# Fifteen loads of 15, 14, ... 1 short rows between the first bulk loads of a decode kernel

## Chip, cores, metric

One core of one Trainium2 chip. The metric is the device time of one execution in microseconds (us); lower is better. A row of numbers for a kernel is the median of its runs. "Landing" is the moment at which one DMA engine reports its part of a load; a load over k engines has k landings, and the trace records each (16 for a 128-row load). The packet records carry no engine number; where an engine is followed, it is by packets that join end to start.

## The reference

One decode step of a transformer block, batch 1, bfloat16: layer norm, attention of one query token over a cache of 4,096 positions in 32 heads of 128, output projection, residual, layer norm, a gated MLP (640 to 1,728 to 640), residual.

```python
h  = x + attention(layernorm(x), k_cache, v_cache, wq, wo)     # k_cache, v_cache: 1 x 32 x 4096 x 128
h2 = h + (gelu(n @ w_gate) * (n @ w_up)) @ w_down              # n = layernorm(h)
```

The inputs are 84.2 MB, each byte used once, so the kernel is a stream of loads with compute behind it.

## The kernel before

All loads are issued by the sync queue (SP), with one semaphore each. The K and V caches come in eight turns of 4 MB each, into two slots. Each of the 16 DMA engines moves eight rows of a 128-row load: at the start of the trace the packets join into sixteen chains of eight rows of 40,960 bytes, eight of 16,384, and so on.

```python
def load(name, dst, src):
    SP.dma_start(dst, src).then_inc(S[name], 16)

def load_kv(which, m, tiles, src, free):      # cut: waits, slot arithmetic
    if (which, m) in (("k", 0), ("k", NQ - 1), ("v", NQ - 1)):
        for h in range(2):                    # in two halves
            r = slice(h * NB // 2, (h + 1) * NB // 2)
            load(f"{which}{slot}{'ab'[h]}", tiles[slot][:, r, :], src[:, r, :])
    else:
        load(f"{which}{slot}a", tiles[slot], src)
# ... cut ...
load("wq", wq_sb, A_wq.rearrange("(p c) n -> p c n", c=DC))            # 128 rows of 40,960 bytes
SP.wait_ge(S["dve"], DVE_X4)
load("x", x4[0:P:32, :], A_x[0, 0].rearrange("(r d) -> r d", r=YR))    # 4 rows of 320 bytes
for m in range(NQ):                           # NQ = 8
    load_k(m)
    if m in (0, 2, 4):
        load_wo(m // 2)                       # 128 rows of 10,240 bytes
    if m == 1:
        SP.wait_ge(S["q"], 1)
    load_v(m)
load_wo(TURNS - 1)
load("wg", wg_sb, B_w_gate.rearrange("(p c) f -> p c f", c=DC))
# ... cut: the up weights in two loads, then the down weights ...
load("wd0", wd_last, B_w_down[FULL * P : DF, :].rearrange("(p b) d -> p b d", b=PER))  # 32 rows
```

At the end GpSimd (POOL) puts the semaphores back, while the output store is under way:

```python
spare(DVE).then_inc(S["all"], 1)
POOL.wait_ge(S["all"], 1)
POOL.sem_inc(S["pe"], -done["pe"])
# ... cut: five more ...
for name in [*once, "x"]:                     # ten names
    POOL.sem_inc(S[name], -16)
ACT.wait_ge(S["out"], 16)
ACT.sem_inc(S["out"], -16)
```

The softmax here doesn't subtract the row's maximum and nothing guards it: scores larger than these inputs give would overflow.

## Time and profile before

| | before |
|---|---|
| time, median of 6 runs | 206.29 us (206.16 to 207.57) |
| span of the profiled run | 204.6 us |
| time after the span's end, same run | 1.65 us |
| 32,768-byte row on one engine, mean | 1.219 us |
| first V load, 16 landings: first / mean / last | 37.58 / 38.00 / 39.57 us |
| last down-projection load, landings: first / mean / last | 199.16 / 200.14 / 201.00 us |
| GpSimd's closing list, first reset to its last no-op | 1.28 us |

The page of the kernel before: the span, its 40 slices of DMA business (tenths) and rate, the packets, two of the queues, and the chain of waits that ended last.

```profile
span 204.6 us, 7392 instructions
...
DMA  7999999999999999999999999999999999999990
GB/s 248 408 420 439 416 471 413 448 434 426 413 416 425 435 426 436 448 429 416 429 436 406 458 442 436 416 423 436 448 429 416 413 423 432 432 420 424 405 366 34
DMA packets 4394, 84.38 MB, mean 412 GB/s; under 512 B 512, under 2 KB 512, under 8 KB 928
...
q1 hardware_dynamic: 4384, 84.23, 96.7%
q8 instruction: 8, 0.13, 0.3%
...
## 4 chain that ended last, share of the span: by engine, by line
DMA 16%; PE 7%; SPq 1%; DVE 0%; issue 0%
DMA big<-in_B_w_down_dram 16%; SPq L510 1%; PE tp_104 L252 1%; PE tp_105 L252 1%; PE tp_106 L252 1%; PE tp_107 L252 1%; PE sa L265 1%; PE sb L265 1%; PE a L288 0%; PE tp_106 L439 0%; DVE y_row L686 0%; PE o L300 0%; DVE spare L169 0%; PE o 
```

The DMA engines are busy in practically every slice, and what the chain of waits ends in is a load. The page's "instruction" queues I take for the program itself being fetched. It goes through the same engines: seven packets of 16 KB between 32 and 76 us took 1.02 to 1.09 us each, and while one is under way fifteen row packets are in flight in place of sixteen.

Stretches of the span, same kernel. Columns: stretch, its length, busy time of five engines with counts, granted clock, DMA share, GB/s.

```profile
...
core 0: us, PE busy (x) PEld busy (x) DVE busy (x) ACT busy (x) POOL busy (x), PEclk, DMA share, GB/s
...
15.00:40.00 25.00, 17.28 (x248) 12.63 (x248) 11.38 (x36) 7.75 (x8) 0.64 (x1) 0.93 1.02 438
40.00:120.00 80.00, 65.41 (x1549) 64.22 (x1545) 28.45 (x55) 38.81 (x88) 8.34 (x4) 0.72 1.00 428
120.00:190.00 70.00, 58.67 (x1514) 56.88 (x1511) 23.56 (x48) 34.73 (x83) 4.49 (x2) 0.73 1.00 429
```

The last column is the one to read: 428 to 438 GB/s in mid-stream.

The end of the chain in order of time (start, duration, what):

```profile
...
168.47 32.53 DMA big<-in_B_w_down_dram
201.00 0.04 issue
201.04 0.47 PE tp_106 L439 x8
201.51 0.02 issue
201.53 0.33 DVE y_row L686
```

The last landing, half a microsecond of matmuls, the add. After that come the output store and the closing handshake. Who ended the sync queue's own waits in that handshake (total, times, longest):

```profile
...
engine line waited for: us in total, times, longest us
...
SPq L158 <- ACTq L158: 0.6, 1, 0.6
```

It is the scalar queue, which waits for the output store. GpSimd's list (1.28 us) is done about 0.45 us sooner and costs nothing.

### The profile page before, as it was taken

Reading aid. Unit: us, or ns where it says so; the run is one execution under the profiler, and the core shown is the slowest. Engines: PE = TensorE matmul, PEld = TensorE weight load, DVE = VectorE, ACT = ScalarE, POOL = GpSimd, SP = SyncE. Lnnn points to the kernel's source line nnn. Section 1 sums busy time; section 2 is a strip of 40 time slices with the busy share of each in tenths; the row PEclk is TensorE's granted clock in tenths of the full one; section 3 lists DMA queues with packets and bytes.
Section 4 is the critical chain, followed back from the end, with each engine's and each line's share of the span. In section 5 each row is a group of like instructions: output and inputs, shape, how many; then the busy total and the mean of one; then the engine's idle time right before and its main releaser. Section 6 shows DMA issues by size and latency. Waiting matters only on the chain. (4 is left out here: it accounts for less than half of the span.)

```text
span 204.6 us, 7392 instructions
## 1 busy us (share of the span) xinstructions
PE 148.9 (73%) x3415; PEld 137.1 (67%) x3415; DVE 71.6 (35%) x180; ACT 81.5 (40%) x179; POOL 19.2 (9%) x17
## 2 busy tenths in 40 slices
PE   0001949945996499889984998199869989986743
PEld 0001239945996499889974997199859979986321
DVE  2006026600471038206601750047107703802660
ACT  0000035543285317535660557027715672870000
POOL 8300000350000000710000035000000000000000
PEclk9999987975597559957975797559757976985575
DMA  7999999999999999999999999999999999999990
GB/s 248 408 420 439 416 471 413 448 434 426 413 416 425 435 426 436 448 429 416 429 436 406 458 442 436 416 423 436 448 429 416 413 423 432 432 420 424 405 366 34
DMA packets 4394, 84.38 MB, mean 412 GB/s; under 512 B 512, under 2 KB 512, under 8 KB 928
## 3 DMA queue, kind: packets, MB, share of 16 engines
q1 hardware_dynamic: 4384, 84.23, 96.7%
q8 instruction: 8, 0.13, 0.3%
q14 instruction: 2, 0.02, 0.0%
HBM read 84.23 MB, written 0.00 MB: 412 GB/s over the span
## 5 line engine op out<-in xcount | busy, mean ns | idle before, releaser
L278 PE MATMUL o<-ex,big 128*128 128x4 bf16 x1024 | 29.9, 166 | 10.1 <-ACT ex L574 6.3
L278 PEld LDWEIGHTS o<-ex,big 128*128 128x128 bf16 x1024 | 28.5, 103 | 11.4 <-ACT ex L574 7.5
L560 ACT COPY big<-tp_105 128x1024 bf16<-128x1024 bf16 x16 | 16.2, 1012 | 46.4 <-PE tp_105 L252 46.4
L252 PE MATMUL tp_104<-ident,big 128*128 128x128 bf16 x256 | 24.1, 250 | 10.6 <-PEq L177 10.6
L252 PEld LDWEIGHTS tp_104<-ident,big 128*128 128x128 bf16 x256 | 19.6, 115 | 11.0 <-issue 11.0
L252 PE MATMUL tp_105<-ident,big 128*128 128x128 bf16 x256 | 24.0, 248 | 0.0
L252 PE MATMUL tp_106<-ident,big 128*128 128x128 bf16 x256 | 23.4, 245 | 0.0
L505 POOL COPY wo<-wo_in 128x5120 bf16<-128x5120 bf16 x3 | 13.4, 4451 | 105.3 <-PE a L288 105.3
L587 DVE COPY big<-tp_104 128x1024 bf16<-128x1024 bf16 x24 | 16.5, 688 | 18.2 <-PE tp_104 L252 18.2
L252 PE MATMUL tp_107<-ident,big 128*128 128x128 bf16 x256 | 22.5, 238 | 0.0
L252 PEld LDWEIGHTS tp_105<-ident,big 128*128 128x128 bf16 x256 | 19.6, 114 | 0.0
L252 PEld LDWEIGHTS tp_106<-ident,big 128*128 128x128 bf16 x256 | 19.3, 113 | 0.0
L252 PEld LDWEIGHTS tp_107<-ident,big 128*128 128x128 bf16 x256 | 18.5, 109 | 0.0
L265 PE MATMUL sb<-q_78,big 128*128 128x4 bf16 x512 | 14.4, 164 | 4.5 <-issue 4.5
L587 DVE COPY big<-tp_107 128x1024 bf16<-128x1024 bf16 x24 | 16.6, 691 | 2.9 <-PE tp_107 L252 2.5
L560 ACT COPY big<-tp_106 128x1024 bf16<-128x1024 bf16 x16 | 16.2, 1014 | 3.3 <-PE tp_106 L252 3.3
L265 PEld LDWEIGHTS sb<-q_78,big 128*128 128x128 bf16 x512 | 13.7, 97 | 4.6 <-issue 4.6
L574 ACT ACTIVATE ex<-sa 32x64 bf16<-32x64 f32 x32 | 9.8, 306 | 11.4 <-PE sa L265 11.2
L587 DVE COPY big<-tp_106 128x1024 bf16<-128x1024 bf16 x16 | 11.1, 692 | 8.4 <-PE tp_106 L252 8.1
L265 PE MATMUL sa<-q_78,big 128*128 128x4 bf16 x512 | 14.0, 164 | 0.0
L265 PEld LDWEIGHTS sa<-q_78,big 128*128 128x128 bf16 x512 | 13.5, 96 | 0.6
L644 DVE COPY o_raw<-o 128x4 f32<-128x4 f32 x4 | 0.7, 163 | 35.8 <-PE o L278 35.8
(118 smaller groups left out, 114.4 us busy)
## 6 DMA issues: line engine op xcount, KB each, us to landing
big<-in_A_v_cache_dram SPq DMA_DIRECT2D x7, 4096.0 KB, 33.0
big<-in_A_k_cache_dram SPq DMA_DIRECT2D x6, 4096.0 KB, 26.6
big<-in_A_k_cache_dram SPq DMA_DIRECT2D x4, 2048.0 KB, 22.0
big<-in_A_wq_dram SPq DMA_DIRECT2D x1, 5120.0 KB, 15.2
wo_in<-in_A_wo_dram SPq DMA_DIRECT2D x4, 1280.0 KB, 25.9
big<-in_A_v_cache_dram SPq DMA_DIRECT2D x2, 2048.0 KB, 28.3
big<-in_B_w_gate_dram SPq DMA_DIRECT2D x1, 2160.0 KB, 37.8
big<-in_B_w_up_dram SPq DMA_DIRECT2D x1, 1728.0 KB, 41.6
```

Source lines behind the costliest of these rows:

```text
L252: inst = PE.transpose(tp_b[g % NBANK][:, b * DH : (b + 1) * DH], kt[slot][:, g * GRP + b, :], ident[:])
L265: inst = PE.matmul(s_ps[half][:, j % (NB // 2), :], lhsT=kt[slot][:, j, :], rhs=q8[:, slot * QH : (slot + 1) * QH], start=True, stop=True,)
L278: inst = PE.matmul(o_ps, lhsT=vt[slot][:, j, :], rhs=e_t[:, j, :], start=(j == 0), stop=(j == NB - 1))
L505: POOL.tensor_copy(wo_t[:], wo_in[:]).then_inc(S["wo"], 1)
L560: ACT.copy(group(m % SLOTS, g), tp_g[g % NBANK]).then_inc(S["act_pe"], 1)
L574: inst = ACT.activation(e_t[r, cols, i], s_ps[half][r, :, i], AF.Exp, scale=SCALE, accum_out=rs_all[r, half, h : h + 1])
L587: DVE.tensor_copy(group(m % SLOTS, g), tp_g[g % NBANK]).then_inc(S["dve_pe"], 1)
L644: event(DVE.tensor_copy(o_raw[:, HG * turn : HG * turn + QH], o_ps))
```

## The change

Fifteen loads, one of 15 rows, one of 14, ... one of 1 row, each row 1,152 bytes, written to scratch space that nobody reads. The intent is a stagger. In the trace of the change a load of k short rows has k landings and one early jump (16 events for 15 rows, 2 for one row), and the loads share their engines: the 42 short packets of the first bunch can be followed as thirteen engines with three of them, one with two, one with one and one with none. Engine e has 15 - e short rows to do and is meant to fall behind by so many steps, so that the engines no longer start their bulk rows together. They stand in four bunches (3, 3, 4 and 5 loads) between the first five bulk loads.

```diff
-        + ["x", "wq", ..., "wd3", "out"]
+        + ["x", "wq", ..., "wd3", "out"] + [f"mark{k}" for k in range(1, 16)]
@@ load_kv
                 load(f"{which}{slot}{'ab'[h]}", tiles[slot][:, r, :], src[:, r, :])
+                if (which, m, h) == ("k", 0, 0):
+                    mark_loads(12, 11, 10)
@@ the order of loads
+    marks = part(2 * SLOTS * TILE + W_MLP, W_MLP)
+
+    def mark_loads(*ks):
+        for k in ks:
+            load(f"mark{k}", marks[0:k, (k - 1) * 576 : k * 576], A_wq[0:k, 0:576])
+
+    mark_loads(15, 14, 13)
     for m in range(NQ):
         load_k(m)
         if m in (0, 2, 4):
+            mark_loads(*{0: (9, 8, 7, 6)}.get(m, ()))
             load_wo(m // 2)
+            mark_loads(*{0: (5, 4, 3, 2, 1)}.get(m, ()))
         if m == 1:
             SP.wait_ge(S["q"], 1)
         load_v(m)
     load_wo(TURNS - 1)
     load("wg", wg_sb, ...)
+    for k in range(1, 16):
+        SP.wait_ge(S[f"mark{k}"], 16)
@@ GpSimd's closing list
-    for name in [*once, "x"]:
+    for name in [*once, "x"] + [f"mark{k}" for k in range(1, 16)]:
+        POOL.wait_ge(S[name], 16)
         POOL.sem_inc(S[name], -16)
```

More of the change, by code (lines that the diff above doesn't have):

```diff
@@ L153 @@
         [f"{t}{i}{h}" for t in "kv" for i in range(SLOTS) for h in "ab"]
-        + ["x", "wq", "wo", "wo_in", "wg", "wu0", "wu1", "wd0", "wd1", "wd2", "wd3", "out"]
+        + ["x", "wq", "wo", "wo_in", "wg", "wu0", "wu1", "wd0", "wd1", "wd2", "wd3", "out"] + [f"mark{k}" for k in range(1, 16)]
         + ["pe", "dve", "act", "pool", "q", "dve_pe", "act_pe", "y", "all"]
```

## The prediction

> **What bounds the kernel now.** The load stream. The page's slices show DMA busy 9 tenths nearly throughout, 412 GB/s on average; the chain of waits ends in 32.5 us of the last down-projection load (16% of the span), then 0.47 us of matmuls, the add and the store. Packet records: a 32,768-byte row takes 1.219 us in the mean, 26.9 GB/s on one engine. [...] In mid-stream each 4 MB load lands 9.72 us after its predecessor, whatever the engines' phases: I see no collision there for a stagger to remove. Excess packet time sits in the first row (about 0.66 us per engine, before any mark), in seven instruction fetches between 32 and 76 us, each setting one engine back by 1.0 us, and at 193 to 196 us (about 0.5 us per engine).
>
> So the engines are spread already: the last load's 16 landings run from 199.16 to 201.00 us, and the last one counts.
>
> **What the change does.** [...] the 4-partition x load agrees: 4 packets, 4 landings and one earlier jump. Loads of 15, 14, ... 1 rows thus give engine 0 fifteen small rows and engine 15 none. One costs, by estimate from rows of 320 (19 ns), 2,560 (102) and 10,240 bytes (385), 50 ns for 1,152 bytes plus 8 ns for the semaphore write: 58 ns. Engine 0 is set back by 0.87 us, engine 8 by 0.4, for good, because the stream never pauses.
>
> Issue: a DMA costs the queue 0.4 to 0.65 us, so fifteen add 7 to 9 us before the first second-slot load (now 4.3 us). The first load alone keeps the engines busy until 15 us, so nothing starves. The fifteen waits before the up weights are long satisfied.
>
> Tail: GpSimd resets semaphores at the end, 0.078 us each, done at 203.2 us; the rest waits for the output store until 203.69. Fifteen more resets cost 1.17 us plus little for waits, so GpSimd ends last, at about 204.4. Less the 0.45 us of slack, about 0.75 us lands on the end.
>
> **On the critical path.** Last landing +0.6 us (one of the lowest four engines already has a fetch and a late start, and gets 0.7 to 0.87 more; the worst engine's number I cannot tell), tail +0.75 us. Sum +1.3 us, 0.6%. The crowding at 193 to 196 us may change by 0.3 us either way.
>
> **Predicted: 207.6 us, range 206.8 to 208.5.** Faster by over 2%: 0.01; within 2%: 0.97; slower: 0.02.
>
> **What would show it.** (a) 120 packets of 1,152 bytes, about 50 ns each. (b) Bulk rows unchanged at 1.219 us, 9.72 us per 4 MB load. (c) Mid-stream landings of one load spread over more than the present 1.8 us, the first landing unmoved. (d) Last down-projection landing near 201.6 us. (e) GpSimd's resets ending 1.2 us later relative to the output add, the closing handshake waiting on GpSimd.
>
> **What would make it wrong.** If the fetches hit high-numbered engines, the ramp evens the engines out and the last landing stays or falls by up to 0.5 us (206.5). If each small load stalls its engine for its semaphore write's round trip (0.4 us from data to landing), engine 0 loses several us: 210. If waits and resets take an instruction each, the tail is 2.5 us longer.

That the stream is the bound rests on the page alone (DMA slices, chain of waits). +0.6 us for the last landing and +0.75 us for the tail make the +1.3 us.

## More of the kernel before

A "completion" is the end of a load's part on one engine, where its semaphore is raised (in the traces a packet of 4 bytes, 9 ns, behind the engine's last row).

## The result

| | before | after |
|---|---|---|
| time, median | 206.35 us (20 runs) | 210.15 us (10 runs, 209.87 to 211.39) |
| span of the profiled run | 204.6 us | 208.8 us |
| time after the span's end, same run | 1.65 us | 2.14 us |
| 32,768-byte row, mean | 1.219 us | 1.219 us |
| first V load, landings: first / mean / last | 37.58 / 38.00 / 39.57 us | 38.52 / 39.46 / 40.59 us |
| last down-projection load, landings | 199.16 / 200.14 / 201.00 us | 200.29 / 201.69 / 203.50 us |
| 1,152-byte row, mean of 120 | none | 107 ns (51 to 336) |
| GpSimd's closing list | 1.28 us | 2.89 us |

The ratio is 1.018, 95% interval 1.016 to 1.020. A ratio is the mean time of one kernel's fast runs over that of the other's fast runs of the same rounds, so it is not quite the ratio of the medians. The change is slower, clear of the noise, by just under 2%. The profiled run (210.90 us) is one of the slower ones of its kernel, 0.75 us over the median.

The page after:

```profile
span 208.8 us, 7429 instructions
...
DMA  6989999999999999999999999999999999999950
GB/s 251 455 358 403 395 450 424 425 433 430 424 436 409 436 419 452 421 427 452 427 404 448 410 458 427 421 433 446 421 433 436 399 430 430 419 433 425 378 217 2
DMA packets 4635, 84.53 MB, mean 405 GB/s; under 512 B 632, under 2 KB 752, under 8 KB 1168
...
q1 hardware_dynamic: 4624, 84.37, 95.5%
q8 instruction: 8, 0.13, 0.3%
...
## 4 chain that ended last, share of the span: by engine, by line
DMA 15%; PE 7%; SPq 1%; DVE 0%; issue 0%
DMA big<-in_B_w_down_dram 15%; SPq L510 1%; PE tp_104 L252 1%; PE tp_105 L252 1%; PE tp_107 L252 1%; PE tp_106 L252 1%; PE sa L265 1%; PE sb L265 1%; PE a L288 0%; PE tp_106 L439 0%; PE o L300 0%; DVE y_row L699 0%; DVE spare L169 0%; PE o 
```

The added packets (241 more, 0.15 MB more) are far too few bytes to account for the loss. Single slices mislead here: the third has fallen from 420 to 358 GB/s, but the second has risen from 408 to 455. Stretches:

```profile
...
core 0: us, PE busy (x) PEld busy (x) DVE busy (x) ACT busy (x) POOL busy (x), PEclk, DMA share, GB/s
...
15.00:40.00 25.00, 16.75 (x243) 12.28 (x244) 11.29 (x36) 7.75 (x8) 0.53 (x1) 0.93 1.02 418
40.00:120.00 80.00, 64.03 (x1503) 62.84 (x1501) 25.89 (x50) 36.85 (x85) 8.45 (x4) 0.70 1.00 428
120.00:190.00 70.00, 59.29 (x1531) 57.90 (x1528) 25.12 (x47) 36.77 (x85) 4.49 (x2) 0.78 1.00 430
```

The loss is in 15 to 40 us alone: 418 for 438 GB/s, and 20 GB/s over 25 us are 0.5 MB, which at 430 GB/s is 1.2 us. From 40 to 190 us the stream runs exactly as before: 428 for 428, 430 for 429. So the stagger costs while it is made and neither gains nor loses later.

The end of the chain, and the waits of the sync queue in the closing handshake:

```profile
...
171.38 32.12 DMA big<-in_B_w_down_dram
203.50 0.04 issue
203.54 0.46 PE tp_106 L439 x7
204.00 0.02 issue
204.03 0.32 DVE y_row L699
```

```profile
...
engine line waited for: us in total, times, longest us
...
SPq L158 <- POOLq L158: 1.2, 1, 1.2
...
SPq L158 <- ACTq L158: 0.5, 1, 0.5
```

The chain has the same links, 2.5 us later (e2 below, profiled at its median, has 1.8 us for the loads alone). But the handshake now waits 1.2 us for GpSimd, which in the kernel before it never waited for. The two losses are separate, a stream loss and a tail loss, and the first experiments divide them.

### The profile page after: what moved, and what is told of

It is laid out like the page before. It is cut to its first block, busy times and chain, and to the rows that moved or that the text cites. A ratio compares the mean times of both kernels' runs of the same rounds, so it can differ in the third digit from the quotient of the medians.

```text
span 208.8 us, 7429 instructions
## 1 busy us (share of the span) xinstructions
PE 148.9 (71%) x3415; PEld 137.4 (66%) x3415; DVE 71.7 (34%) x180; ACT 81.6 (39%) x179; POOL 19.2 (9%) x17
## 5 line engine op out<-in xcount | busy, mean ns | idle before, releaser
L310 PE MATMUL o<-x_col,mean_f 128*128 128x10 f32 x2 | 0.6, 376 | 17.2 <-DVE x_col L208 17.2
```

Of the source, the lines that this page charges most:

```text
L310: mark("moments", PE.matmul(ps, lhsT=mean_f[:], rhs=rhs, start=True, stop=True))
```

## The experiments

Eighteen kernels, each timed in five rounds against the kernel before; all gave correct results. By times alone none is 2% slower than the kernel before (at most 1.4%, e6), and the 95% interval of a ratio is about 0.7 us to either side. Finer differences are therefore read from landings, of one profile per kernel. "d" is the median less the median of before. Landings are quoted as first / mean / last of 16. In the texts of expectation a kernel is named without its number.

A note on the times. Every kernel, the one before included, has a second group of runs about 1.1 us above the first (before: mostly 206.1 to 206.9, some at 207.5 to 208.0). In most profiles of slower runs the last thing to finish is not the load but the compute behind it: in e9, e11, e13, e14, e16 and e18 the output add starts 1.3 to 2.8 us after the last landing, in all the others 0.4 to 0.5 us. The change's own profile is an exception: it is 0.75 us over the median with an add 0.53 us after the last landing, so there the landings themselves were late. The chain of e13_own8_four, whose profile fell in the upper group, reads

```profile
...
## 4 chain that ended last, share of the span: by engine, by line
PE 15%; DVE 4%; ACT 4%; issue 1%
PE tp L252 9%; ACT ex L593 4%; PE o L278 2%; PE sa L265 2%; PE tp L439 1%; PE a L288 1%; DVE g_col L669 0%; DVE u_col L669 0%; PE tp L310 0%; PE tp L300 0%; DVE h_col L207 0%; DVE rs_w L221 0%; DVE rs_w L222 0%; DVE rs_y L224 0%; PE o L300 
```

with TensorE's granted clock at 0.50 from 190 to 200 us, and no DMA in the chain's summary. The clock is not shown to be the cause: it is 0.50 there in e10's profile too, which is of the lower group. No profile of the kernel before fell into its upper group, so that its runs there are the same thing is inferred. Where a median hops between groups (e13, e16), I compare landings or the groups, not medians.

### Dividing tail and stream: e1_resets_only, e2_loads_only

e1 leaves the fifteen loads out and raises their semaphores by hand; e2 keeps the loads and resets their semaphores on the sync queue.

```diff
# e1                                              # e2
     def mark_loads(*ks):                              for k in range(1, 16):
-        for k in ks: load(...)                            SP.wait_ge(S[f"mark{k}"], 16)
+        pass                                     +    for k in range(1, 16):
+    for k in range(1, 16):                       +        SP.sem_inc(S[f"mark{k}"], -16)
+        SP.sem_inc(S[f"mark{k}"], 16)            # GpSimd's closing list as before
```

> The fifteen loads are left out; their semaphores are raised by the sync queue at about 153 us instead, and the longer list of waits and resets at the end of GpSimd stays. If the tail and the stream are separate terms, this costs the tail alone: in the changed kernel GpSimd's list took 2.89 us against 1.28, less about 0.45 us of slack, so +1.2 us, 207.5 us, with the last down-projection landing still near 201.0 us and its spread 1.8 us. Rival: the longer tail is an accident of the profile (0.4 us of it was a late sync drain) and the time moves by the +0.75 us of the prediction or less, 207.1 us.

> The fifteen loads stay as they are; their semaphores are reset by the sync queue after its fifteen waits at about 154 us, and GpSimd's end is that of the kernel before. The stream's share alone: last landing near 203.5 us instead of 201.0, so +2.3 to +2.6 us, 208.8 us. Together with the resets alone it should make the whole +3.8 us. If the prediction's 58 ns a load were right and the rest were tail, it would be 207.0 us.

Measured: e1 208.66 us (d +2.17), last landing 201.25; e2 208.12 us (d +1.63), landings of the first V load 38.42 / 39.40 / 40.59, last landing 202.83. 2.17 + 1.63 = 3.80, and the whole change costs 210.15 - 206.35 = 3.80. The two terms add (to the hundredth by luck: e2's six runs reach from 207.70 to 208.75), and the tail is the larger. The waits of the sync queue in the handshake, e1 and then e2:

```profile
...
SPq L158 <- POOLq L158: 1.2, 1, 1.2
```

```profile
...
SPq L158 <- ACTq L158: 0.6, 1, 0.6
```

Both texts missed the sizes: e1 cost 1 us more than I had worked out of the profile, e2 0.7 us less. What the profile of the span could not show is that e1's runs also end later after the span: 2.21 us on average against 1.70 of before, and 1.67 in e2.

### The tail: e8_pool_early, e16_resets_padded

```diff
# e8: GpSimd, after its third copy at about 115 us, not in the closing list
+    for k in range(1, 16):
+        POOL.wait_ge(S[f"mark{k}"], 16)
+        POOL.sem_inc(S[f"mark{k}"], -16)
+    spare(POOL).then_inc(S["pool"], 1)
# ... and the sync queue, in place of its fifteen waits
+    SP.wait_ge(S["pool"], POOL_ALL)
# e16: e1 and, on the sync queue at about 154 us,
+    for _ in range(15):
+        SP.sem_inc(S["mark1"], 1)
+        SP.sem_inc(S["mark1"], -1)
```

> The fifteen loads as in the change; GpSimd waits for and resets their semaphores after its third copy (about 115 us) instead of at the end, then tells the sync queue, which waits once. If the tail's +2.2 us came from GpSimd's list standing at the end, it is gone: 208.1 us as with the loads alone, and the time after the last counted instruction is 1.6 us again, not 2.2. If it came from GpSimd's program being longer [...], it stays: 209.5 us or more.

> resets_only (208.66 us) with thirty more semaphore instructions on the sync queue at about 154 us, where it has time. Fetch theory [...]: the extra fetch of 8 KB moves to about 160 us, the drain that came 0.46 us late comes at once, the time after the last counted instruction is 1.65 us again: 207.6 us. If the lateness comes from GpSimd being last: unchanged, 208.66 us.

Measured: e8 208.78 us, 0.66 above e2 rather than 2.0, so most of the tail goes when the list is moved, but not all: its runs still end 2.04 us after the span. e16 has a median of 209.36 us, in the upper group; its two runs of the lower group are 207.89 and 208.01 us against 208.57 to 208.67 of e1's lower group. From the traces (us):

```
                        GpSimd's list   late drain of SP   time after the span, mean
before                      1.28             0.06               1.68 to 1.71
after                       2.89             0.46               2.17
e1_resets_only              2.89             0.46               2.21
e2_loads_only               1.28             0.06               1.67
e8_pool_early               1.27             0.06               2.04
e16_resets_padded           2.89             0.06               2.17
```

Three pieces, then. (1) The list: 25 steps of 0.096 us instead of 10 of 0.078, +1.61 us, less about 0.45 us of slack, is +1.15. (2) One drain of the sync queue in the handshake starts 0.46 us after the step before it instead of 0.06. Padding that queue's program by thirty instructions in mid-run removes this, and an extra fetch of 8 KB of instructions appears at 159 us instead (it also stands in e2, at 159 us, where the drain is prompt). So it depends on how long the program is; I take it for a fetch at an unlucky place, but no fetch packet is recorded in the gap itself. (3) The time after the span is 0.34 us (e8) to 0.51 us (e1) longer in the four kernels whose GpSimd program is longer, and in none of the others, wherever in the program the addition stands. Sum for e1 1.15 + 0.40 + 0.51 = 2.06 of the measured 2.17. That (3) too is fetching of instructions is argued from the fetch packets after the span (two in before, three or four in these), not shown.

### What a short row costs: e3 to e7

All on e2. e3: row i to partition 9i, no longer to adjacent partitions. e4: rows read from wo. e5: rows cut to 32 bytes. e6: all fifteen loads with 16 rows. e7: the rows of e6 in four loads.

The theories in the texts are guesses. "Source" says that it matters which rows are read, "completion" how many loads end on an engine, "port" and later "foreign-port" which partitions the rows are written to. Read "port" as a name alone.

```diff
-            load(f"mark{k}", marks[0:k, (k - 1) * 576 : k * 576], A_wq[0:k, 0:576])
+e3                           marks[0 : 9 * k - 8 : 9, (k - 1) * 576 : k * 576], A_wq[0:k, 0:576]
+e4                           marks[0:k, (k - 1) * 576 : k * 576], A_wo[0:k, 0:576]
+e5                           marks[0:k, (k - 1) * 576 : (k - 1) * 576 + 16], A_wq[0:k, 0:16]
+e6                           marks[0:16, (k - 1) * 576 : k * 576], A_wq[0:16, 0:576]
+e7  (4 loads, n = 3,3,4,5)   [16 partitions, n rows of 576], A_wq[0:16, 0 : n * 640] as n rows
```

> As the loads alone, but the k rows of a load go to partitions 0, 9, 18, ... instead of 0, 1, 2, ...: same engines, same rows, same bytes[...]. Port theory [...]: small rows fall from a mean of 107 ns to near 51, the rows after them return to 0.61 us, last landing near 201.7 us, 207.0 us. Source theory or completion theory: nothing changes, 208.8 us.

> As the loads alone, but the rows are read from wo, whose rows lie 1,280 bytes apart, instead of wq, whose rows lie 8,192 apart. Source theory [...]: small rows fall to near 51 ns, last landing near 201.7 us, 207.0 us. Port theory or completion theory: nothing changes, 208.8 us.

> As the loads alone (208.1 us, +1.6), but each row is cut from 1,152 bytes to 32. Completion theory (what costs is that a load ends on an engine, whatever it carried): nearly the whole delay stays, 207.5 to 208.1 us, and the bulk rows behind a group of small loads are still slowed. Bytes theory (what costs is the extra rows' traffic): next to nothing is left, 206.7 us.

> As the loads alone, but each of the fifteen loads has 16 rows, so that every engine gets fifteen small rows and fifteen completions. At the prediction's 58 ns each this is +0.9 us for every engine, 207.4 us. Completion theory: at the 0.15 to 0.19 us a small load that landings in a row were apart, +2.3 to +2.9 us, 209 us.

> The same rows and bytes as fifteen_by_16, but in four loads of 16 partitions and 3, 3, 4 and 5 rows each: four completions per engine instead of fifteen. Completion theory: 15 rows at 50 ns plus four completions, +0.8 to +1.2 us, 207.4 us, clearly below its twin. Bytes theory: the same time as fifteen_by_16.

| | time | d | first V load, landings | 1,152-byte rows, mean |
|---|---|---|---|---|
| e2_loads_only | 208.12 | +1.63 | 38.42 / 39.40 / 40.59 | 70 ns |
| e3_spread_dst | 208.10 | +1.61 | 38.29 / 39.32 / 40.51 | 102 ns |
| e4_near_src | 207.81 | +1.32 | 38.93 / 39.57 / 40.65 | 53 ns |
| e5_tiny | 207.89 | +1.39 | 38.10 / 39.10 / 40.74 | (32 bytes) |
| e6_fifteen_by_16 | 209.50 | +3.00 | 40.60 / 40.95 / 42.43 | 69 ns |
| e7_four_by_16 | 209.27 | +2.77 | 40.58 / 40.96 / 42.48 | 64 ns |

The mean landing is the best measure: 38.00 us in before. e2 loses 1.40 us per engine by it, over 120 rows on 16 engines: 1.40 x 16 / 120 = 0.19 us of engine time for each row. e6 and e7 lose 2.95 us for 15 rows on each engine: again 0.19 to 0.20. The prediction had 0.058.

These figures rest on one profile per kernel, and part of each arose before the first short row: the wq load, which stands ahead of all of them, lands at 15.31 us in the mean in before, at 15.40 to 15.42 in e1, e16 and e18 (no early short loads) and at 15.35 to 15.65 in the others. With each kernel's own lateness of wq taken off, e2 loses 1.20 us (0.16 us a row), e6 and e7 2.75 and 2.62 (0.17 to 0.18 us a row): still about three times the forecast.

Each theory alone failed here. Partitions: e3 changed nothing (mean landing 39.32 us for 39.40). Source rows: e4 made the short rows fast (53 ns), but the bulk rows behind them slower (16,384-byte rows 647 ns instead of 636, before 611), and the delay stayed. Bytes: e5, with 32 bytes a row, lost 1.10 us instead of 1.40; the difference, 0.04 us a row, is what the 1,152 bytes themselves take (51 ns less 9). Completions: e7, with four completions for fifteen, cost as much as e6.

The landings gave the clue. In e9 (below) the last bunch's five loads, one row each on an engine, have their earliest landings at

```
29.54  29.73  29.92  30.12  30.32
```

0.195 us apart, whereas a row's data take 51 ns (all 120 rows of e13 below). In e9's first bunch all 24 rows did take 51 ns, and their landings, compared rank by rank, are 0.18 to 0.22 us apart all the same. In its later bunches the rows themselves become long (over all 120 a mean of 133 ns, at most 334), and that is where the engine's time goes; the semaphore writes, recorded as packets of 4 bytes, stay at 9 ns. With 32 bytes a row (e5) the first landings of neighbouring loads are 0.16 to 0.21 us apart in the first three bunches. What sets this distance the traces do not show. And e7, with four completions for fifteen, still wrote to adjacent partitions (0 to 15), while e3, with partitions nine apart, still had all its completions. Two limits of the same size, one in completions and one in adjacent partitions, would hide each other: taking one away leaves the other. At this point that was a guess.

### Two limits: e9 to e14

Now all loads but e12's have 8 rows (engines 0 to 7), fifteen rows per engine. e9: row i to partition 4i. e10: row i to partition i ("near"). e13 and e14: the same two with the rows in four loads. e11: e10 with rows from far places, none read twice. e12: two loads of 128 rows.

```diff
+e9   marks[0:32:4, ...], A_wq[0:8, 0:576]      # fifteen loads
+e10  marks[0:8, ...],    A_wq[0:8, 0:576]      # fifteen loads
+e11  marks[0:8, ...],    K cache rows 128 KB apart, new columns for each load
+e12  marks[:, 0:576], A_wq[0:128, 0:576] and marks[:, 576:1152], A_wq[128:256, 0:576]
+e13  [partitions 0:32:4, n rows of 576]        # four loads, n = 3, 3, 4, 5
+e14  [partitions 0:8,    n rows of 576]        # four loads
```

> Loads alone, all fifteen of 8 rows, row i to partition 4i[...]. Foreign-port theory [...]: about 58 ns a row, engines 0 to 7 set back by 0.9 us, v landings of the first slot about 0.4 us later in the mean. Row theory (a short row between long ones costs about 0.19 us wherever it lands) and hot-rows theory (fifteen loads read the same few rows): engines 0 to 7 set back by 2.8 us, mean +1.4 us.

> The same with the 8 rows in partitions 0 to 7[...]. Foreign-port theory: engines 0 to 7 set back by 2.8 us, mean +1.4 us, so clearly over own8. Row theory and hot-rows theory: the same as own8.

> As near8, but every row of every load is read from its own place in the K cache (128 KB apart, and new columns for each load), none twice. Hot-rows theory: the delay goes, mean +0.4 us. Row theory and foreign-port theory: as near8, mean +1.4 us.

> Two loads of 128 rows of 1,152 bytes (one after wq and x, one behind the two halves of K), every engine 16 rows[...]: the same number of short rows per engine as fifteen_by_16, which was set back by 2.9 us. Foreign-port theory and hot-rows theory: 16 rows at 58 ns, +0.9 us. Row theory: +2.9 us again.

> The rows of own8 (8 rows, [...]15 per engine) in four loads of 3, 3, 4 and 5 rows per engine instead of fifteen loads. If completions in a row are the cost there: engines 0 to 7 are set back by 15 x 0.05 = 0.8 us instead of 2.7, mean of the first v load +0.4 us, 207.3 us. If a short row costs 0.18 us by itself: +2.7 us again, 209.5 us.

> The same four loads with rows in partitions 0 to 7[...]. Port theory: [...]15 rows still set engines 0 to 7 back by about 2.5 us and the others are disturbed too, 208.7 us as near8. If ports do not matter once completions are few: as own8_four, 207.3 us.

| | partitions | loads | time | first V load, landings | mean less 38.00 |
|---|---|---|---|---|---|
| e9_own8 | four apart | 15 | 209.50 | 37.92 / 39.39 / 40.84 | +1.39 |
| e13_own8_four | four apart | 4 | 208.11 | 37.83 / 38.50 / 39.59 | +0.50 |
| e10_near8 | adjacent | 15 | 208.67 | 38.89 / 39.84 / 40.97 | +1.84 |
| e14_near8_four | adjacent | 4 | 209.29 | 38.98 / 39.79 / 40.70 | +1.79 |
| e11_cold8 | adjacent | 15 | 208.67 | 38.98 / 39.91 / 41.12 | +1.91 |
| e12_full128 | all 128 | 2 | 208.60 | 38.92 / 40.06 / 41.78 | +2.06 |

The stretch 15 to 40 us of e9, e13, e10 and e14, in this order (last column GB/s; before 438):

```profile
...
15.00:40.00 25.00, 17.20 (x233) 13.20 (x234) 11.36 (x36) 7.84 (x8) 0.27 (x1) 0.86 1.01 412
```

```profile
...
15.00:40.00 25.00, 17.19 (x252) 12.57 (x253) 11.38 (x36) 7.74 (x8) 0.75 (x1) 0.93 1.02 435
```

```profile
...
15.00:40.00 25.00, 17.24 (x249) 13.50 (x250) 11.38 (x36) 7.84 (x8) 0.67 (x1) 0.86 1.01 412
```

```profile
...
15.00:40.00 25.00, 16.99 (x236) 12.35 (x237) 11.37 (x36) 7.75 (x8) 0.36 (x1) 0.93 1.02 412
```

Only where both are taken away, the adjacent partitions and the completions in a row, in e13, does the rate come back (435). There all 120 short rows took 51 ns, and the bulk rows behind them 611 ns as in before. If the eight engines without short rows are untouched, as the next paragraph shows for e9, +0.50 in the mean is 1.0 us for each of the other eight: 15 rows at 51 ns (0.77 us) and little else; with the 0.15 us by which wq landed late taken off it is 0.70 us, the rows' data alone. e9 cost those engines 2.7 us; the eleven completions more are worth 1.7 us (1.9 with wq taken off in both), 0.15 to 0.18 us each.

Following the packets of each engine in the trace of e9, engines 0 to 7 are set back by 2.3 to 2.95 us, and seven of the other eight by 0.4 us or less, most of them not at all (the eighth, 1.5 us back, had an instruction fetch, whose packet took 0.93 us). In e10 engines 8 to 15, which have no short row at all, are set back by 1.1 us; the table shows it too: e10's first landing is at 38.89 us, by which time 15 of the 16 landings of the kernel before were in. So short rows in adjacent partitions cost every engine here, while in e9, with completions in a row, the engines without a short row stay within 0.4 us but for the one with the fetch. How rows in adjacent partitions hold up an engine that moves none of them I cannot tell from these traces.

e11 speaks against hot rows: far-apart rows, none read twice, cost the same as e10, and its landings in a bunch are as far apart (0.20 to 0.21 us in the mean). It does not exclude them where the partitions are four apart: e11 has the adjacent partitions, which may hide the difference, and e9 and e13 differ in what they read as well (e9 the same eight pieces fifteen times, e13 three to five neighbouring pieces of eight rows in each load). e9 with rows from far places was not run, so that completions make the difference between e9 and e13 is argued from the landings, not isolated. That adjacent partitions do is shown: e13 and e14 differ in the partitions alone (mean landing +0.50 against +1.79 us).

e12 is half a surprise. Its second load came as predicted: its landings follow those of the load before it by 0.34 to 0.39 us, eight rows at 46 ns. Its first load, right behind wq and x, took 0.5 to 1.9 us for the same eight rows. Why those were slow stays open; the very first rows of wq, which all engines also begin together, are slow too in every kernel (2.1 to 2.3 us in the mean, later rows 1.52).

### The change's own loads, and a hunch about the kernel before: e15, e17, e18

e15 puts one of the change's loads behind each of fifteen bulk loads. e17 does that with row i in partition 9i. e18 is the kernel before with its one load that goes to 32 partitions (wd0, rows of 2,560 bytes) moved from 193 us to behind K's second turn.

```diff
# e15, in load(); e17 with marks[0 : 9 * k - 8 : 9, ...]
         SP.dma_start(dst, src).then_inc(S[name], 16)
+        if not name.startswith("mark") and name != "wq":
+            k = next(order, None)                        # 15, 14, ... 1
+            if k:
+                load(f"mark{k}", marks[0:k, (k - 1) * 576 : k * 576], A_wq[0:k, 0:576])
# e18
-    wd_last = part(FULL * D, PER * D)[0:HP]...
+    wd_last = sb("wd_last", [P, PER * D], bf16)[0:HP]...
+        if m == 1:
+            load("wd0", wd_last, ...)
```

> The change's fifteen loads (15, 14, ... 1 rows, partitions from 0 on), one behind each of fifteen bulk loads instead of in bunches of three to five; resets as in loads_only. Completions in a row and crowding in time are both gone but for a single load's rows: 58 ns for each, engine 0 set back by 0.9 us over the run, last landing about +0.5 us, 207.0 us. If each small load costs 0.18 us wherever it stands: as loads_only, 208.1 us.

> As apart, but row i of a load goes to partition 9i[...]. [...]the prediction's 58 ns a row holds at last: 120 rows make a mean of 0.44 us per engine (apart had +1.4), engine 0 is 0.9 us back, last landing about 201.6 us, 206.9 us. If something else costs 0.18 us a row: as apart, 207.7 us.

> The kernel before, with the 32-row load of the down projection's last rows (2,560 bytes each, partitions 0 to 31[...]) moved from 193 us to behind the second slot's first load, into a tile of its own. Port theory: the 10,240-byte rows that follow at 193 to 196 us go back from a mean of 437 ns towards 385 to 400, and the stream's end comes up to 0.4 us earlier, less what the load now costs where it stands: 205.9 to 206.5 us. If the crowding has another cause, the rows stay at 437 ns.

The first figures of e17's text are for the case that completions in a row and adjacent partitions are the whole loss.

The fifth V load has fourteen of the fifteen short loads ahead of it (119 of the 120 rows); its mean landing is 122.53 us in before. e15: 207.73 us, 123.90 (+1.37), no better than e2 there (123.93). e17: 207.37 us (d +0.80), 123.46 (+0.93); all short rows at 51 ns. So partitions nine apart help once the loads stand apart, as the two-limit reading says, but 0.44 us was expected for 120 rows at 58 ns and 0.93 came. Half a microsecond (0.3 with the lateness of wq taken off) is still unexplained. One rival was not tested: e17's partitions are nine apart, e13's four, and e17 was not run with four. In that trace the first rows of the bulk loads at 25 and 28 us are up to 0.2 us slow. The stretch 15 to 40 us of e17:

```profile
...
15.00:40.00 25.00, 17.19 (x255) 12.62 (x256) 11.34 (x36) 7.75 (x8) 0.83 (x1) 0.93 1.01 429
```

e18: 206.60 us (d +0.03). The stretch 193 to 197 us, before and then e18:

```profile
...
193.00:197.00 4.00, 3.56 (x45) 1.45 (x37) 3.25 (x17) 0.21 (x1) 0.00 (x0) 0.53 1.01 365
```

```profile
...
193.00:197.00 4.00, 3.09 (x29) 1.45 (x33) 2.82 (x16) 0.00 (x0) 0.00 (x0) 0.50 0.99 416
```

416 for 365 GB/s, and the 10,240-byte rows after 190 us are back from 437 to 385 ns, the shortest that the kernel before has. So the crowding at 193 to 196 us that the prediction had noticed goes with that load. But the fifth V load's mean landing is 0.94 us later (123.47), and the end the same: the cost moved with the load, and nothing was gained. No kernel tried here beats the kernel before.

## Why the prediction was wrong

Right, by the runs:
- What bounds the kernel, and that no collision was there to remove: bulk rows at 1.219 us before and after, 428 to 430 GB/s from 40 to 190 us in both.
- Which engines run a small load. The 8-row loads show nine landing events, eight and one early jump, in e9 the set-back engines are eight, and the first bunch of the change has thirteen engines with three short rows and one each with two, one and none.
- That issue costs nothing: e2, with all fifteen issues, starves no engine (DMA share 1.01 from 15 to 40 us).
- That GpSimd would end last, and that the two terms add.

Wrong, in the prediction's words:
- "One costs ... 58 ns". The row's data took 51 ns, as estimated, where nothing was in its way (e13, e17). But each short row cost about 0.19 us of engine time (e2, e6; 0.16 to 0.18 with the lateness of wq taken off). Short rows in adjacent partitions are shown to cost about that much (1.29 us more in the mean landing of e14 than of e13, over 120 rows 0.17 us each); completions in a row, 0.15 to 0.18 us each, are the reading of e9 against e13, with hot rows not excluded there. The estimate came from the shortest rows within single loads of the kernel before (19, 102 and 385 ns), where neither limit shows. The x load, one small row, had cost 0.03 us, which says nothing of three to five in a row.
- "Engine 0 is set back by 0.87 us" and no other engine by more than its own rows: rows in adjacent partitions set back even engines without a short row (1.1 us, e10). Together: stream +1.63 us (e2), forecast +0.6.
- "Fifteen more resets cost 1.17 us plus little for waits". The waits were given to the ten old resets too, and a step with a wait takes 0.096 us for 0.078: +1.61 us. Two costs were not in the sum at all: a drain 0.40 us later that goes with the length of the sync queue's program (e16), and 0.3 to 0.5 us after the span that goes with GpSimd's (e1, e8, e16). Together: tail +2.17 us (e1), forecast +0.75.
- Of its five tests, (b) held. (a) The 120 packets came, with a mean of 107 ns for 50. (c) The third V load's landings do spread more (1.8 us before, 3.3 after), but the first is not unmoved: 79.64 us before, 80.51 after. (d) 203.50 us for 201.6. (e) The handshake waits for GpSimd, whose list ends 1.6 us later for 1.2.

The prediction named the right danger in its last paragraph, a stall per small load "for its semaphore write's round trip", and gave it too little weight, as it had seen only bulk loads pass from one to the next without a gap (0.01 us, the semaphore write included). The size was not that round trip (0.4 us) but about half of it.

## What to carry to other kernels

In this kernel a small load between large ones was not priced by its bytes: ask how many completions an engine has in a row, and whether the rows of one load go to adjacent partitions. If a short transfer must be there, put its rows four partitions apart in few loads: that cost least here (e13, +0.50 us in the mean landing). And count a closing list step by step, since what stands idle there before the change may be last after it; divide a loss into its terms (resets alone, loads alone) before explaining any of it.
